# A fused gated linear attention and expert layer: the hand-laid instruction orders of its first half are laid out anew

## The chip, the core and the metric

The program runs on one core of a Trainium2 chip. The metric is the device time of one execution in microseconds (us), the median of several executions. The core has a matrix engine (TensorE, PE), a vector engine (VectorE, DVE), an activation engine (ScalarE, ACT), GpSimd (POOL) and a queue engine (SyncE, SP) that issues DMA transfers. Each takes its own instructions strictly in the order in which the program gives them, so an instruction that waits holds back all that stand behind it on its engine.

## What is computed

A gated linear attention (4 batches, 8 heads, 768 steps, head size 48) is followed by a top-1 mixture of 8 experts over the 3072 resulting tokens:

```python
mag = np.sqrt(a_re * a_re + a_im * a_im)
scale = np.minimum(mag, 0.999) / (mag + 1e-06)
a_re_n, a_im_n = (a_re * scale, a_im * scale)
for t in range(S):
    new_re = ar * S_re - ai * S_im
    new_im = ar * S_im + ai * S_re
    kv = np.einsum('bhd,bhe->bhde', k[:, :, t], v[:, :, t])
    S_re, S_im = (new_re + kv, new_im)
    y[:, :, t] = np.einsum('bhd,bhde->bhe', q[:, :, t], S_re)
...
logits = x @ w_gate
e_idx = np.argmax(logits, axis=1)
eom = 1.0 / (1.0 + np.exp(-(x @ w_output_gate)))
for e in range(E):
    mask = e_idx == e
    h = np.maximum(x[mask] @ w1[e], 0.0)
    ye = h @ w2[e]
    out[mask] = gate_w[mask, None] * eom[mask, e, None] * ye
```

## The kernel before

The kernel has two stages. **Attention and routing** work through 24 chunks of 128 tokens, six of each batch; loads and the elementwise preparation go by ten groups of 1, 1, 2, 2, 3, 3, 3, 3, 3, 3 chunks. **The experts** follow: eight of them, each with up-projections (`L1521`), a rectifier (`L1525`, `L1526`), down-projections (`L1453`, `L1479`) and the splitting of the next expert's float32 weights in a high and a low part (`L376`, `L377`).

Everything in the first stage is an operation with a name, a key (kind and chunk, `scores.21`), entered with `add_op` together with its engine and the keys that must come before it. The string `ORDER` lists all names once, and `Flow.go` emits them in that sequence; it asserts that each operation's predecessors have been emitted and that its PSUM bank is free. An engine's own order is the sequence of its names in `ORDER`. `=N` and `+N` in it put N idle multiplications on PE that compute nothing. The semaphores between the engines are derived from the data.

The names that matter, by chunk `i` or routing batch `n`:

- `scaled.i.k`, `scaled.i.q` (DVE `L783`) multiply keys and queries by the decays `ri`, `re`; `rotated.i.k`, `rotated.i.q` (DVE `L880`, tiles `kc`, `qc`) turn them by the phase. Those have two inputs in SBUF. `phase.i`, `whole.i`, `part.i`, `carry.i` sum up the phase angles from chunk to chunk (PE `L830`, `L833`; DVE `L837`, `L864`, `L823`).
- `half.i.k.0` and the like (PE `L252` on `kc`, `qc`) transpose one half of these, `copied` (ACT `L893`) empties the bank.
- `scores.i` (PE `L951`) is the product of queries and keys, `masked.i` (DVE `L957`) masks it, `values.i` (PE `L974`, `L981`) multiplies by the values and by the state of the chunk before, `xt.i` (ACT `L987`) empties that bank, `rows.i` (PE `L252` on `xt`) transposes back and `xn.i`, `stored.i` write the rows to DRAM.
- `state.i` (PE `L920`), `summed.i` (DVE `L928`), `carried.i` (POOL `L931`) carry the state on.
- `gates.m` and its steps 1 to 3 give a pair of chunks its gate logits: PE `L408`, ACT `L412`, PE `L252` on `ls`, DVE `L418`.
- The routing goes in batches of 8, 8 and 4 chunks (n = 0, 1, 2), the last four chunks apart as `place` and `place_two`. `choose.n`, `choose2.n` (DVE) find the expert of each token, `ranks.n` (PE `L455`) counts, `ranked.n` (DVE `L457`, `L459`, tile `found`) gives each token its rank, `exps.n` and `weighed.n` (ACT, then DVE `L480` to `L483`, tile `entry`) its weight. `hot.c` (`L539`) marks the ranks of chunk c, on POOL for batch 0 and on DVE afterwards. `cut.n` and `product.n` (POOL `L545` to `L552`, tiles `parts`, `rest`, `many`) split the entries, and `listed.n`, `listed.n.1` (PE `L559`) add up the two halves of a batch into one PSUM bank, which `held.n` empties.
- After batch 2, `spread` (PE `L569`), `slots` (DVE `L575`) and `first_ids` (DVE `L1360`) give the rows of the first expert, which `gather.0` to `gather.3` (POOL, DMA, `L1382`) fetch and `identity.0` to `identity.3` (PE `L1212`) transpose. `fill` and `last` (PE `L1196`) add the last four chunks; then the first up-projection starts.
- `split.0` to `split.5` (ACT and DVE) split the first weights, `raw.0` to `raw.8` load them (SP).

Of the kernel before, what the change touches and what calls it, by code (L numbers as in the profile page):

```python
# [40 lines left out]
    arctan.3 phase.2 whole.1 halves.1 v.5 wg.1 kinds part.1 k.6 magnitude.0 =3 carry.2 magnitude.1 q.6 cosine.0 sine.1
    phase.3 v.6 whole.2 cosine.1 part.2 rotated.0.q ar.6 sine.2 =3 carry.3 ai.6 magnitude.2 phase.4 whole.3 ar.7
    half.0.q.0 part.3 ai.7 half.0.q.1 copied.0.q.0 rotated.0.k ar.8 carry.4 copied.0.q.1 sine.3 ai.8 half.0.k.1
    whole.4 cosine.2 phase.5 copied.0.k.1 part.4 k.7 magnitude.3 sine.4 q.7 =1 carry.5 magnitude.4 cosine.3 ratios.0
    cosine.4 whole.5 half.0.k.0 state.0 copied.0.k.0 part.5 scores.0 sine.5 magnitude.5 scaled.1.q cosine.5
    rotated.1.k rc.0 load.1 carried.0 state.1 masked.0 half.1.k.0 ln2.2 ratios.1 summed.1 values.0 copied.1.k.0 sum.2
    half.1.k.1 rotated.1.q scale.2 k.8 copied.1.k.1 bound.2 +2 half.1.q.1 xt.0 half.1.q.0 q.8 count.2 ln2.3 decay.2
    v.7 copied.1.q.1 sum.3 ar.9 ri.2 rows.0 rc.1 ai.9 copied.1.q.0 scaled.2.k xn.0 ar.10 count.3 scores.1 ln.4 ai.10
    rotated.2.k ar.11 re.2 ai.11 inverse.4 masked.1 carried.1 +1 half.2.k.1 stored.0 decay.3 copied.2.k.1 ratio.4
    scale.3 values.1 ri.3 bound.3 square.4 scaled.2.q v.8 decay.4 xt.1 scaled.3.k ar.12 ln2.4 rotated.2.q gates.0  # L50
    ai.12 rotated.3.k row.2 k.9 gates.0.1 half.2.q.1 re.3 half.2.k.0 copied.2.q.1 sum.4 row.3 ar.13 copied.2.k.0
    half.2.q.0 ri.4 ai.13 half.3.k.0 copied.2.q.0 decay.5 ar.14 scaled.3.q scale.4 scaled.4.k ai.14 rows.1 rotated.3.q
    q.9 scores.2 ri.5 copied.3.k.0 bound.4 re.4 xn.1 row.4 half.3.k.1 re.5 half.3.q.0 scaled.4.q copied.3.k.1 decay.6
    copied.3.q.0 masked.2 halves.2 ln.5 half.3.q.1 ratios.2 q.10 rotated.4.q values.2 copied.3.q.1 row.5 stored.1
    inverse.5 count.4 ri.6 half.4.q.0 xt.2 ratio.5 state.2 copied.4.q.0 re.6 scores.3 v.9 rc.2 rotated.4.k square.5
    k.10 scaled.5.k half.4.k.1 summed.2 halves.3 ln2.5 decay.7 scaled.5.q k.11 half.4.q.1 scaled.6.q row.6 ri.7
    decay.8 scaled.6.k q.11 copied.4.q.1 sum.5 re.7 ri.8 row.7 ratios.3 copied.4.k.1 masked.3 carried.2 re.8 state.3
    scale.5 row.8 half.4.k.0 rotated.5.q gates.0.2 values.3 copied.4.k.0 load.1.5 summed.3 rotated.5.k rc.3 count.5
    half.5.q.0 arctan.4 v.10 rows.2 copied.5.q.0 bound.5 phase.6 xn.2 xt.3 state.4 arctan.5 whole.6 carried.3 scores.4
    gates.0.3 part.6 carry.7 gates.1 summed.4 masked.4 phase.7 gates.1.1 carried.4 sine.6 half.5.k.0 magnitude.6  # L60
    half.5.k.1 whole.7 halves.4 cosine.6 values.4 part.7 copied.5.k.1 sine.7 carry.8 copied.5.k.0 scaled.7.k
    magnitude.7 rotated.6.k phase.8 xt.4 rows.3 cosine.7 whole.8 half.5.q.1 xn.3 ratios.4 part.8 copied.5.q.1 q.12
    rows.4 scaled.8.k rc.4 magnitude.8 v.11 half.6.k.0 carry.9 sine.8 scores.5 k.12 rotated.6.q copied.6.k.0 stored.2
    cosine.8 rotated.7.k xn.4 stored.3 phase.9 load.2 masked.5 half.6.q.0 half.6.k.1 copied.6.q.0 decay.9 whole.9 ln.6
    half.6.q.1 scaled.7.q values.5 part.9 q.13 copied.6.k.1 rotated.7.q k.13 copied.6.q.1 inverse.6 stored.4 carry.10
# [66 lines left out]
    identity.0 identity.1 identity.2 identity.3 fill.20 place_two high.23 place_two.0 low.22 place_two.1 fill.21  # L132
    place_two.2 low.23 piece.3 place_two.3 place_two.4 hot.20 hot.21 hot.22 hot.23 tail_exps last.0 last.1 xn.22 xn.23
    first_high.0 first_low.0 last.2 first_high.1 first_low.1 first_up.0 first_high.2 first_up.1 first_low.2 stored.22
    tail_gates cut.3 product.3 first_up.2 stored.23
"""


# [1644 lines left out]
```

## Time and profile before

| what | value |
|---|---|
| median of 3 runs | 476.84 us (475.33 to 477.55) |
| profiled execution, its own time | 477.41 us |
| its span, first to last instruction | 475.2 us |
| mean granted clock of TensorE | 0.988 |
| busy: PE, DVE, ACT, POOL | 452.8, 373.5, 301.0, 131.7 us |

2.2 us lie outside the span. Times in the rows are counted from the span's start. A row of the timeline has the start, the length, engine, line, operation, tiles and, in brackets, how long the engine stood idle ahead of it and whom it waited for. A row of the windows has the length of a stretch, then each engine's busy time in it with its instructions, the granted clock (1.00 is the level of 2.4 GHz, 0.50 that of 1.2 GHz) and the load of the DMA engines.

### The profile page before, as it was taken

Reading aid. Unit: us, or ns where it says so; the run is one execution under the profiler, and the core shown is the slowest. Engines: PE = TensorE matmul, PEld = TensorE weight load, DVE = VectorE, ACT = ScalarE, POOL = GpSimd, SP = SyncE. Lnnn points to the kernel's source line nnn. Section 1 sums busy time; section 2 is a strip of 40 time slices with the busy share of each in tenths; the row PEclk is TensorE's granted clock in tenths of the full one; section 3 lists DMA queues with packets and bytes.
Section 4 is the critical chain, followed back from the end, with each engine's and each line's share of the span. In section 5 each row is a group of like instructions: output and inputs, shape, how many; then the busy total and the mean of one; then the engine's idle time right before and its main releaser. Section 6 shows DMA issues by size and latency. Waiting matters only on the chain.

```text
span 475.2 us, 13763 instructions
## 1 busy us (share of the span) xinstructions
PE 452.8 (95%) x5634; PEld 391.8 (82%) x5634; DVE 373.5 (79%) x716; ACT 301.0 (63%) x580; POOL 131.7 (28%) x169
## 2 busy tenths in 40 slices
PE   8998989999999999989899999999999999999992
PEld 7765767777776777768778899999999999999992
DVE  4799999999997999973867587595886859597540
ACT  6879989999997997644444553553626445463231
POOL 5300410023932231124014051704226060410232
PEclk9999999999999999988999999999999999999998
DMA  8946516454442220025834846373552837310111
GB/s 277 292 132 205 183 52 183 138 171 134 135 149 87 72 86 20 32 89 129 272 107 114 280 120 198 86 238 104 182 158 57 279 95 229 108 38 0 51 40 57
DMA packets 45436, 63.91 MB, mean 134 GB/s; under 512 B 10365, under 2 KB 37200, under 8 KB 45364
## 3 DMA queue, kind: packets, MB, share of 16 engines
q1 hardware_dynamic: 38132, 53.55, 35.9%
q0 software_dynamic: 7232, 9.39, 7.4%
q8 instruction: 46, 0.75, 0.7%
q14 instruction: 26, 0.21, 0.2%
HBM read 53.83 MB, written 9.77 MB: 134 GB/s over the span
## 4 chain that ended last, share of the span: by engine, by line
PE 68%; DVE 19%; ACT 5%; issue 3%; POOL 2%; DMA 2%; SPq 0%; POOLq 0%; DVEq 0%; ACTq 0%
PE up L1521 23%; PE acc L1453 20%; PE tr L252 4%; PE sx L974 3%; DVE scores L957 3%; PE sx L951 3%; PE cs L830 2%; PE sx L981 2%; DVE kc L880 2%; PE xt L252 2%; DVE qc L880 1%; PE acc L1479 1%; DMA ar<-in_a_re_blocks_dram 1%; PE tr L920 1%; DVE l L743 1%
## 5 line engine op out<-in xcount | busy, mean ns | idle before, releaser
L1525 ACT ACTIVATE hh<-up 128x384 fp32r<-128x384 f32 (+6 forms) x64 | 32.9, 513 | 91.5 <-PE up L1521 89.8
L1526 DVE SCALAR_TENSOR_TENSOR hl<-up,hh 128x384 fp32r<-128x384 f32 (+6 forms) x64 | 37.3, 583 | 46.9 <-ACT hh L1525 46.5
L1521 PE MATMUL up<-xh,w1h 128*128 128x384 f32 (+6 forms) x192 | 68.5, 357 | 0.0
L1521 PE MATMUL up<-xl,w1h 128*128 128x384 f32 (+6 forms) x192 | 67.2, 350 | 0.0
L1521 PE MATMUL up<-xh,w1l 128*128 128x384 f32 (+6 forms) x192 | 67.1, 350 | 0.0
L1382 POOL DMA_INDIRECT rows<-xd,sid x28 | 35.4, 1264 | 96.3 <-PE xt L252 78.1
L1453 PE MATMUL acc<-hh,w2h 128*128 128x464 f32 (+6 forms) x168 | 59.0, 351 | 0.0
L1453 PE MATMUL acc<-hl,w2h 128*128 128x464 f32 (+6 forms) x168 | 58.9, 351 | 0.0
L1453 PE MATMUL acc<-hh,w2l 128*128 128x464 f32 (+6 forms) x168 | 58.9, 351 | 0.0
L1466 POOL DMA_INDIRECT out_dram<-y,sid x28 | 31.5, 1125 | 48.2 <-ACT y L1491 43.3
L1487 DVE COPY y<-yt 32x384 f32<-32x384 f32 x112 | 39.8, 355 | 1.9
L951 PE MATMUL sx<-qt,kt 32*128 32x128 f32 x1152 | 39.0, 279 | 0.3 <-ACT xt L987 0.2
L951 PEld LDWEIGHTS sx<-qt,kt 32*128 32x128 f32 x1152 | 34.4, 187 | 3.3 <-issue 1.4
L1521 PEld LDWEIGHTS up<-xh,w1h 128*128 128x128 f32 x192 | 36.1, 188 | 1.1 <-issue 0.4
L1521 PEld LDWEIGHTS up<-xh,w1l 128*128 128x128 f32 x192 | 36.2, 188 | 0.8
L1521 PEld LDWEIGHTS up<-xl,w1h 128*128 128x128 f32 x192 | 36.1, 188 | 0.8
L931 POOL TENSOR_TENSOR state<-summed,rc 128x288 f32<-128x288 f32 x16 | 16.1, 1006 | 72.9 <-DVE summed L928 31.9
L377 DVE TENSOR_TENSOR w1l<-raw,w1h 128x512 fp32r<-128x512 f32 x48 | 30.4, 683 | 6.7 <-ACT w1h L376 6.5
L1453 PEld LDWEIGHTS acc<-hl,w2h 128*128 128x128 f32 x168 | 31.6, 188 | 0.9
L1453 PEld LDWEIGHTS acc<-hh,w2l 128*128 128x128 f32 x168 | 31.6, 188 | 0.8
L1453 PEld LDWEIGHTS acc<-hh,w2h 128*128 128x128 f32 x168 | 31.6, 188 | 0.8
L377 DVE TENSOR_TENSOR w2l<-raw,w2h 128x512 fp32r<-128x512 f32 x48 | 30.2, 683 | 0.2
(230 smaller groups left out, 1036.1 us busy)
## 6 DMA issues: line engine op xcount, KB each, us to landing
raw<-in_moe_w_dram SPq DMA_DIRECT2D x29, 768.0 KB, 5.4
ar<-in_a_re_blocks_dram SPq DMA_DIRECT2D x24, 192.0 KB, 4.2
ai<-in_a_im_blocks_dram SPq DMA_DIRECT2D x24, 192.0 KB, 3.4
k<-in_k_blocks_dram SPq DMA_DIRECT2D x24, 192.0 KB, 2.6
q<-in_q_blocks_dram SPq DMA_DIRECT2D x24, 192.0 KB, 4.1
v<-in_v_dram SPq DMA_DIRECT2D x24, 192.0 KB, 2.4
xd<-xn SPq DMA_DIRECT2D x24, 192.0 KB, 2.9
raw<-in_moe_w_dram SPq DMA_DIRECT2D x6, 256.0 KB
```

The costliest lines, as they stand in the source:

```text
L252: return nc.tensor.transpose(out=out, in_=in_, identity=ident[p0:p0 + n, p0:p0 + n])
L377: ins = nc.vector.tensor_tensor(out=lo[:, s], in0=raw[:, s], in1=hi[:, s].bitcast(F32), op=ALU.subtract)
L880: nc.vector.tensor_tensor(out=dst, in0=n3(at(i, n)).unsqueeze(2).broadcast_to([P, NB, 2, DB]), in1=at(i, "trig"), op=ALU.mult)
L931: return lambda: engine.tensor_tensor(out=states[cc % 2], in0=of(), in1=rc[:, i, :].unsqueeze(2).broadcast_to([P, GB, D]), op=ALU.mult)
L951: r["end", "scores"] = nc.tensor.matmul(r["sx"][:, b, u * P:(u + 1) * P], kt, qt, start=(j == 0), stop=(j == JB - 1), skip_group_check=True)
L1382: nc.gpsimd.indirect_dma_start(out=rows[0][:n, i, :], out_offset=None, in_=xd[:known], in_offset=bass.IndirectOffsetOnAxis(ap=ids[:n, i:i ...
L1453: nc.tensor.matmul(accs[kt][:, :cap], w[:, cs], a, start=(ft == 0 and s == 0), stop=(ft == FT - 1 and s == 2))
L1466: ins = nc.gpsimd.indirect_dma_start(out=out, out_offset=bass.IndirectOffsetOnAxis(ap=ids(e)[:n, i:i + 1], axis=0), in_=y[:n, :], in_offse ...
L1487: nc.vector.tensor_copy(out=y[SQ * g:SQ * g + SQ, :, QD * a:QD * a + QD], in_=yt[SQ * a:SQ * a + SQ, :, g, :])
L1521: nc.tensor.matmul(up[:, :cap], w[:, kt, :], x[kt], start=(m == 0), stop=(m == 3 * KT - 1))
L1525: nc.scalar.activation(out=hh, in_=up[:, :cap], func=AF.Relu)
L1526: nc.vector.scalar_tensor_tensor(out=hl, in0=up[:, :cap], scalar=0.0, in1=hh.bitcast(F32), op0=ALU.max, op1=ALU.subtract)
```

## The change

`ORDER` is replaced by another sequence of the same names: no operation is added, removed or given to another engine, apart from the idle multiplications (16 in all become 22). SP's own order stays the same, name by name. DVE, ACT, PE and POOL get new ones. One predecessor is added, which only fixes the order of `identity.0` to `identity.3` among themselves.

```diff
 ORDER = """
-    warm.0 load.0 ar.0 ai.0 ar.1 ln.0 ai.1 inverse.0 ratio.0 ar.2 square.0 ai.2 ln.1 ar.3 ln2.0 ai.3 inverse.1 sum.0
...
+    warm.0 load.0 ar.0 ai.0 ar.1 ln.0 ai.1 inverse.0 ratio.0 ar.2 square.0 ai.2 ln.1 ar.3 inverse.1 ai.3 ln2.0
...
                 for i in range(len(tiles)):
                     add_op(("identity", i), "PE", 0.08 * KT, due, lambda i=i: gathered(i), [
-                        ("gathered", i), ("xt", NT - 1)])
+                        ("gathered", i), ("xt", NT - 1), *([("identity", i - 1)] if i else [])])
```

Lines of the changed kernel are two higher: `L559` becomes `L561`. Three places stand here engine by engine. The first is PE at `listed.2`, the sums of the last routing batch (`many`, `hot`), before:

```order
L252 MATMUL tr<-ident,xt 128x128 x4
L920 MATMUL tr<-v,kc_174 32x48 x24
L951 MATMUL sx<-qt_180,kt_181 128x128 x24
L559 LDWEIGHTS many
L559 MATMUL cs<-hot,many 40x464
```

In the kernel before, `listed.2` stands right behind `scores.21`. On PE at the same place now:

```order
L953 MATMUL sx<-qt_180,kt_181 128x128 x24
L254 MATMUL tr<-ident,qc_171 128x128 x3
L254 MATMUL tr<-ident,xt 128x128 x4
L254 MATMUL tr<-ident,kc_172 128x128 x3
L976 MATMUL sx<-scores,v 48x128 x8
L983 MATMUL sx<-qt_180,state_175 48x128 x24
L254 MATMUL tr<-ident,kc_172 128x128 x3
L254 MATMUL tr<-ident,qc_171 128x128 x3
L561 LDWEIGHTS many
L561 MATMUL cs<-hot,many 40x464
```

Between them now stand the four halves of chunk 22, `rows.19` and `values.21`. The second place is DVE at the same batch, from `ranked.2` (`of`, `found`) on, before:

```order
L459 TENSOR_REDUCE found<-of 128x8
L539 TENSOR_SCALAR hot<-iota,found 128x464 x4
L480 TENSOR_REDUCE sm<-ex 128x4
L481 TENSOR_SCALAR en<-en 128x4
L482 SCALAR_TENSOR_TENSOR en<-sm,en 128x4
L483 RECIPROCAL entry<-en 128x4
L928 TENSOR_TENSOR summed<-tr,state_175 128x288
L880 TENSOR_TENSOR kc_172<-k,trig 128x768
L957 TENSOR_TENSOR scores<-sx,mask_91 128x1024
```

And DVE there now:

```order
L461 TENSOR_REDUCE found<-of 128x8
L541 TENSOR_SCALAR hot<-iota,found 128x464 x2
L930 TENSOR_TENSOR summed<-tr,state_175 128x288
L959 TENSOR_TENSOR scores<-sx,mask_91 128x1024
L541 TENSOR_SCALAR hot<-iota,found 128x464
L482 TENSOR_REDUCE sm<-ex 128x4
L483 TENSOR_SCALAR en<-en 128x4
L484 SCALAR_TENSOR_TENSOR en<-sm,en 128x4
L485 RECIPROCAL entry<-en 128x4
L541 TENSOR_SCALAR hot<-iota,found 128x464
L882 TENSOR_TENSOR qc_173<-q,trig 128x768
L882 TENSOR_TENSOR kc_174<-k,trig 128x768
```

`weighed.2`, which gives POOL the entries for `cut.2`, now stands behind `summed.21` and `masked.21`, and both rotations of chunk 23 follow it. The third place is PE at the two halves of the first batch's sum, `listed.0` and `listed.0.1`, before (the transposition of `ls` is `gates.5.2`):

```order
L559 MATMUL cs<-hot,many 40x464
L830 MATMUL cs<-ai,tri_t_85 128x384
L252 MATMUL tr<-ident,qc_171 128x128 x3
L252 MATMUL tr<-ident,xt 128x128 x4
L559 LDWEIGHTS many
L559 MATMUL cs<-hot,many 40x464
...
L252 MATMUL cs<-ident,ls 128x128
L974 MATMUL sx<-scores,v 48x128 x8
```

The same two halves on PE now:

```order
L561 MATMUL cs<-hot,many 40x464
L410 MATMUL tr<-xt,wg 32x128 x8
L922 MATMUL tr<-v,kc_174 32x48 x24
L976 MATMUL sx<-scores,v 48x128 x8
L254 MATMUL tr<-ident,qc_173 128x128 x3
L254 MATMUL tr<-ident,kc_172 128x128 x3
L832 MATMUL cs<-ai,tri_t_85 128x384
L922 MATMUL tr<-v,kc_172 32x48 x24
L953 MATMUL sx<-qt_180,kt_181 128x128 x24
L254 MATMUL tr<-ident,kc_172 128x128 x3
L561 LDWEIGHTS many
L561 MATMUL cs<-hot,many 40x464
```

`listed.0` has moved ahead of `gates.5`, `values.12` and `scores.13`, which now lie between the halves, and `gates.5.2` has moved far behind them, to just ahead of `values.14`. On POOL, `hot.5` now stands behind `product.0`, and `carried.13` between `hot.6` and `hot.7`.

## Rows read from the trace of the kernel before

**Rows 1.** Windows of three stretches: length, busy time of each engine, clock, DMA.

```profile
30.00:201.20 171.20, 163.81 (x3528) 123.56 (x3520) 165.98 (x272) 155.29 (x294) 43.37 (x41) 1.00 0.38 115
140.00:150.00 10.00, 9.23 (x185) 6.21 (x181) 7.28 (x12) 7.69 (x14) 3.68 (x4) 1.00 0.14 43
240.60:475.00 234.40, 225.52 (x1253) 217.89 (x1251) 162.30 (x333) 105.03 (x206) 68.51 (x63) 0.99 0.42 126
```

**Rows 2.** Timeline around the last routing batch, up to the first up-projection.

```profile
201.21 1.21 DVE L957 TENSOR_TENSOR scores<-sx,mask 128x1024 f32<-128x1024 f32 x1
...
205.33 0.22 DVE L459 TENSOR_REDUCE found<-of 128x8 f32<-128x64 f32 x1
...
207.18 0.44 DVE L928 TENSOR_TENSOR summed<-tr,state 128x288 f32<-128x288 f32 x1
207.32 0.20 POOL L545 CAST parts<-entry 128x4 bf16<-128x4 f32 x1 [7.89 <-DVE entry L483]
207.53 0.95 DVE L880 TENSOR_TENSOR kc<-k,trig 128x768 f32<-128x768 f32 x1
207.60 0.94 POOL L546 TENSOR_TENSOR rest<-entry,parts 128x4 f32<-128x4 f32 x1
...
209.68 0.96 PE L559 MATMUL cs<-hot,many 128*40 128x464 bf16 x4 [1.92 <-POOL many L552]
...
218.94 1.62 PE L951 MATMUL sx<-qt,kt 32*128 32x128 f32 x48
...
225.72 1.62 PE L951 MATMUL sx<-qt,kt 32*128 32x128 f32 x48
...
227.75 1.21 DVE L957 TENSOR_TENSOR scores<-sx,mask 128x1024 f32<-128x1024 f32 x1
...
240.46 0.38 PE L1521 MATMUL up<-xh,w1h 128*128 128x464 f32 x1
```

**Rows 3.** Windows at that wait, behind it and at a later one.

```profile
208.00:210.00 2.00, 0.32 (x2) 0.22 (x3) 1.62 (x2) 0.00 (x0) 1.78 (x5) 1.00 0.82 256
211.00:218.00 7.00, 6.93 (x83) 5.60 (x80) 2.43 (x5) 1.82 (x4) 2.03 (x2) 0.51 0.00 0
228.00:230.00 2.00, 0.98 (x16) 0.83 (x16) 2.00 (x3) 2.00 (x4) 0.00 (x0) 1.00 0.45 160
```

**Rows 4.** Timeline of DVE near 145 us: its two longest waits there.

```profile
145.10 0.29 DVE L418 TENSOR_REDUCE logits<-cs 128x32 f32<-128x128 f32 x1 [1.33 <-PE cs L252]
...
148.13 0.56 DVE L837 TENSOR_SCALAR rnd<-cs 128x384 f32<-128x384 f32 x1 [1.00 <-PE cs L830]
```

**Rows 5.** Timeline of PE and DVE ahead of the sum of the first routing batch.

```profile
136.08 0.65 PE L408 MATMUL tr<-xt,wg 128*32 128x128 f32 x16
...
138.79 1.62 PE L951 MATMUL sx<-qt,kt 32*128 32x128 f32 x48
...
140.69 1.22 DVE L957 TENSOR_TENSOR scores<-sx,mask 128x1024 f32<-128x1024 f32 x1
```

**Rows 6.** Timeline of POOL in the first routing batch: its first and last operation.

```profile
115.64 4.35 POOL L539 TENSOR_SCALAR hot<-iota,found 128x464 bf16<-128x464 f16 x2 [8.23 <-DVE found L459]
...
131.48 1.70 POOL L552 TENSOR_TENSOR many<-oh,parts 128x320 bf16<-128x320 bf16 x1
```

**Rows 7.** Timeline: the same steps of POOL and PE at other places.

```profile
171.80 0.42 POOL L545 CAST parts<-entry 128x8 bf16<-128x8 f32 x1 [2.28 <-DVE entry L483]
...
174.71 0.72 POOL L552 TENSOR_TENSOR many<-oh,parts 128x320 bf16<-128x320 bf16 x1
...
242.80 0.20 POOL L546 TENSOR_TENSOR rest<-entry,parts 128x4 f32<-128x4 f32 x1
...
248.19 0.98 PE L569 MATMUL yp<-perm,sums 40*116 40x16 f32 x8
```

**Rows 8.** Timeline row of the last gather, and the tile view's landing times of all four.

```profile
221.13 1.32 POOL L1382 DMA_INDIRECT rows<-xd,sid  x1 [0.30 <-issue]
...
DMA to landing us min/median/max: 6.3/6.9/8.0
```

More of the change, by code (lines that the diff above doesn't have):

```diff
@@ L41 @@
[L41 to L65, printed above, removed]
@@ L81 @@
-    scaled.12.q ranks.0 copied.11.k.0 rotated.11.q ri.14 state.10 xt.9 ranked.0 hot.0 hot.1 rows.8 re.14 summed.10
-    exps.0 bound.7 half.11.k.1 xn.8 scores.10 load.3.5 k.18 count.7 row.13 v.16 copied.11.k.1 q.17 gates.4 sine.12
-    row.14 stored.8 masked.10 carried.10 phase.14 gates.4.1 cosine.12 half.11.q.0 arctan.7 half.11.q.1 whole.14
-    values.10 scaled.13.k copied.11.q.0 part.14 halves.6 hot.2 hot.3 hot.4 hot.5 copied.11.q.1 sine.13 carry.15
-    magnitude.14 rotated.12.k rows.9 xt.10 phase.15 xn.9 rotated.12.q sine.14 half.12.k.1 stored.9 half.12.k.0
@@ L116 @@
-    half.20.q.0 magnitude.22 scaled.22.q rows.17 ri.23 count.9 copied.20.q.0 scores.19 re.23 xn.17 load.6.5 carried.19
-    stored.17 half.20.k.1 masked.19 hot.14 hot.15 row.23 state.20 listed.1.1 copied.20.k.1 phase.23 sine.21 summed.20
-    held.1 ranking.2 half.20.q.1 cosine.21 half.20.k.0 copied.20.q.1 values.19 whole.23 sine.22 rotated.21.q
-    copied.20.k.0 order scaled.23.q gates.8.2 xt.19 half.21.q.0 part.23 rows.18 copied.21.q.0 gates.8.3 scores.20
-    magnitude.23 rotated.21.k xn.18 sine.23 scaled.23.k stored.18 halves.9 half.21.q.1 masked.20 carried.20 gates.9
@@ L131 @@
-    place.2 +3 gates.11 place.3 rows.22 gates.11.1 place.4 gates.11.2 rows.23 high.22 gates.11.3 fourth gathered.3
[L132 to L135, printed above, removed]
+    warm.0 load.0 ar.0 ai.0 ar.1 ln.0 ai.1 inverse.0 ratio.0 ar.2 square.0 ai.2 ln.1 ar.3 inverse.1 ai.3 ln2.0
@@ new lines @@
+    summed.10 ranks.0 rotated.11.q xt.9 half.11.k.1 re.14 half.11.k.0 ranked.0 k.18 copied.11.k.1 scores.10 carry.14
+    exps.0 hot.0 row.13 v.16 copied.11.k.0 bound.7 load.3.5 q.17 half.11.q.0 row.14 hot.1 rows.8 masked.10
+    copied.11.q.0 phase.14 arctan.7 half.11.q.1 whole.14 values.10 halves.6 weighed.0 sine.12 carried.10 xn.8
+    part.14 cosine.12 hot.2 scaled.13.k stored.8 copied.11.q.1 carry.15 ratios.6 sine.13 gates.4 rotated.12.k rc.6
+    phase.15 cosine.13 hot.3 gates.4.1 rows.9 rotated.12.q xt.10 gates.4.2 half.12.k.0 xn.9 whole.15 hot.4 scores.11
@@ new lines @@
+    half.13.k.0 decay.17 copied.13.k.0 part.16 square.8 half.13.q.0 scaled.15.k listed.0 masked.12 copied.13.q.0
+    gates.5 ri.17 hot.6 scaled.15.q state.13 ln2.8 carry.17 values.12 summed.13 gates.5.1 re.17 sum.8 half.13.q.1
+    xt.12 half.14.k.0 carried.13 copied.13.q.1 phase.17 magnitude.15 count.8 hot.7 state.14 scale.8 scores.13
+    summed.14 copied.14.k.0 rotated.14.q load.4.5 half.14.k.1 masked.13 listed.0.1 k.21 copied.14.k.1 sine.15 v.19
+    half.14.q.0 whole.17 held.0 values.13 row.16 row.17 bound.8 q.20 copied.14.q.0 cosine.15 stored.11 arctan.8
@@ L136 @@
+    first_low.2 hot.20 first_up.2 tail_gates hot.21 cut.3 hot.22 hot.23 product.3
 """
```

149 lines of the change are left out of this document (90 added, 59 removed).

## The prediction

> **What bounds the kernel now.** I read the windows first. From 240.6 us to 475.0, the experts, PE is busy for 225.5 of 234.4 us at full clock [rows 1]. Nothing in that stage is reordered, so what the change does to the time is what it does to the moment at which the first up-projection starts, 240.46 us [rows 2]. Ahead of that, the windows tell two regimes. From 30 to 201.2 us DVE works for 165.98 of 171.20 us, PE for 163.81, ACT for 155.29 [rows 1]: three engines nearly full, DVE the fullest, with 5.2 us of idle time. 2.7 of these lie in one stretch, 140 to 150 us, where DVE works for 7.28 us. Behind 201.2 us DVE is no longer the bound. The timeline there shows one large disturbance: PE stands 1.92 us at `listed.2`, waiting for POOL's `many` [rows 2]. In the window of that wait PE is busy for 0.32 of 2.00 us, and in the 7 us from 211 to 218 its clock is 0.51, the level of 1.2 GHz [rows 3]. A pause of about 1 us at 228 us had no such consequence: the clock stayed 1.00 [rows 3].
>
> **The change part by part.** No operation is added, apart from six idle multiplications, and none changes its engine or its form. SP's order is the same name by name, so no transfer is issued past another one on that queue. The sum is therefore one of waits that go, move or appear.
>
> *Start-up.* The same DVE operations stand ahead of the third group's bound, in another sequence, and a chain through PE and DVE sets the pace there. I take 0, with half a microsecond to either side.
>
> *The middle, up to `masked.20` at 201.21 us.* I compared the DVE operations that stand ahead of it: they are the same set before and after. The work is the same, so only idle time can differ: at most 5.2 us can be gained [rows 1]. I look for what happens to the two largest waits. DVE waits 1.33 us for the transposition of the gate logits `ls`, and 1.00 us for `phase.18` [rows 4]. Both came from the first batch's sum: `gates.5.2` needs a PSUM bank that `listed.0` holds until POOL has made `hot.6` and `hot.7`, and PE stands in order. Now `gates.5.2` follows far behind, and over 6 us of other PE work lies between the two halves of that sum, against two `hot` of at most 2.2 us each [rows 6] and one `carried`. Both waits should go: -2.3 us.
>
> What comes late next is `scores.13`. It started at 138.79 us and its mask at 140.69 [rows 5]. `listed.0` now stands just ahead of `gates.5`, which started at 136.08; with slightly less ahead of it I put it at 135.7. Up to `scores.13` PE then has 0.9 (`listed.0`), 0.6, 0.7, 1.0, two halves of 0.4, 0.8 (`phase.17`) and 0.7 (`state.14`), together 5.3 us: start 141.0, end 142.6. DVE, with 0.7 us more in front, comes to `masked.13` at 141.4 and would wait 1.2 us. So the middle brings -2.3 + 1.2 = -1.1 us. The ends: -5.2, if no idle time were left, and +2, if `scores.13` is late by the whole 3 us of work moved ahead of it and nothing absorbs that.
>
> *The end, from 201.21 us.* DVE first. Between `masked.20` and the end of `ranked.2`, at 205.55 [rows 2], one rotation of 0.87 us is now added, and a wait of 0.16 us goes: 206.25. Two `hot` (0.5), `summed.21` (0.4) and `masked.21` (1.15) bring it to 208.3, a third `hot` and `weighed.2` (0.9) to 209.2; before, POOL could start at 207.32 [rows 2]. The five POOL operations of `cut.2` and `product.2` took 2.3 us, from 207.32 to 209.62. The same kind took 3.63 us for batch 1, from 171.80 to 175.43 [rows 7]. They now run beside two rotations with two SBUF inputs, as `rest` did when it took 0.94 us beside `kc` [rows 2] and not the 0.20 of a quiet moment [rows 7]. I take the middle, 3.0 us: `many` is there at 212.2, between 211.5 and 212.9.
>
> PE does not stand still all that time. `values.21` now precedes `listed.2`: it can start when `masked.21` ends, at 208.3, and takes 1.9 us; with the two halves behind it PE reaches `listed.2` at 211.1. The wait is 0.4 to 1.8 us, 1.1 as I take it. By the pause at 228 us that is short enough for the clock to stay [rows 3].
>
> Then PE has 0.9 us of `listed.2`. The stretch from `scores.22` at 218.94 to `scores.23` at 225.72, 6.78 us without a wait [rows 2], holds the work that now lies between `listed.2` and `scores.23`, but for `spread`, 0.98 us at full clock [rows 7], and two more halves, 0.9. That makes 0.9 + 6.78 + 0.98 + 0.9 = 9.55, and `scores.23` starts at 212.2 + 9.45 = 221.65 against 225.72: 4.1 us earlier. Its mask started 2.03 us later, at 227.75 [rows 2], because DVE stood behind the choice of the tail; now it can start 1.6 us later: 4.5 us earlier. From there to the first up-projection PE is full in both orders, with the same work. Only `gather.3` may come late: it followed `slots` by some 6 us and landed 6.3 to 8.0 us behind its issue [rows 8], so it is there at about 230.5 and `identity.3` is reached at 230.3. I charge 0.3 us and keep 1.4. The end brings -4.2 us; its ends are -5.2 (short POOL chain) and -2.5 (long chain, late gather).
>
> Two moves cost nothing, and this is what hides them. `kinds` on POOL now stands ahead of `hot.0`; POOL waited 8.23 us there [rows 6]. The gate exponentials and the marks of the last four chunks now stand behind the first up-projection's inputs; POOL's `rest` at 242.80 shifts by some 0.4 us, and PE needs the result only near 246 us. If that cover were gone, it would cost the same 0.4 us.
>
> *The sum.* 0 - 1.1 - 4.2 = -5.3 us. Against the profiled execution's own 477.41 us that is 472.1. The median of the runs, 476.84, lies 0.57 us lower, so by it 471.5. I put down 471.8.
>
> **The rivals.** *The stop at `listed.2` stays.* If both rotations block POOL, each by the 0.74 us between 0.94 and 0.20, the chain takes 2.3 + 1.5 = 3.8 us and PE waits 1.9 us: the wait after which the clock fell. The low clock cost half of 7 us, 3.5, and the wait another 0.8, so that the end gains nothing: about 476. For it speaks that `weighed.2` is now later and the rotations follow it at once; against it, that batch 1, in the full middle, took 3.63. The Trainium skill says in "SBUF — State Buffer", section "Who interferes with whom", that a VectorE instruction with two SBUF inputs and a GpSimd instruction that reads SBUF exclude each other for the whole instruction. By that rule this rival would be the rule here; the trace agrees in `rest`, 0.94 beside `kc` and 0.20 alone, and no row shows the two rotations together.
>
> *The middle gives back what the end gains.* PE has only 7.4 us of idle time from 30 to 201.2 us [rows 1], and the new order asks for much of its work earlier. Two more waits like the one at `masked.13`, at 1.2 to 2 us each, leave -5.3 + 3 = -2.3: about 475. Against it: the waits shown are few, and DVE's sequence is close to the old one.
>
> *Slower: the stop moves to `listed.0`.* It now stands ahead of `gates.5`, `values.12` and `scores.13`. POOL needs its ten operations before it, 115.64 to 133.2, 17.5 us [rows 6]; PE comes at 135.7. From 20 us of POOL on, PE stands with all of that behind it. A stop of 4 us, a fall of the clock as at `listed.2`, 3.5 us, and the end's gain of 4.2 make 480.7. Against it: POOL's operations are the same, with 2.5 us in hand.
>
> *It does more.* If DVE's idle time in the middle nearly vanishes, -5.2 and -4.2 give 467.7.
>
> **How the numbers follow.** Forecast 0.55, stop stays 0.17, middle gives back 0.13, slower 0.08, more 0.07. Half a per cent, 2.4 us, is about what a measurement of this kernel can tell from no change. Faster by more than that: 0.55 + 0.07 + half of the middle's, 0.06, is 0.68. Within it: 0.17 + 0.07 = 0.24. Slower: 0.08. The range leaves out the slower case and half of the best one: 467.5 to 477.0.
>
> **What would show it.** The step at `listed.2` is right if PE's wait for `many` is under 1.5 us and no window from 200 to 240 us shows a clock under 0.95; `scores.23` then starts 4 us earlier and the first up-projection near 235. The step in the middle is right if the waits at `gates.5.3` and `whole.18` are gone, `masked.13` waits for PE about 1 us, and `masked.20` starts near 200. The experts must take 234.7 us again. It is wrong if `masked.20` starts later than 202, if POOL's chain takes over 3.7 us, or if PE waits at `identity.3` or at `listed.0`.

## The result, and the profile after

The changed kernel takes 470.5 us (median of 4 runs, 470.06 to 470.96) against 476.97 of the kernel before in the same comparison: a ratio of 0.987, 95% interval 0.9843 to 0.9897, or 6.5 us less. In a second comparison (below, `after_again`) the ratio is 0.986, interval 0.982 to 0.989. The forecast was 471.8, with 467.5 to 477.0 around it.

The profiled execution took 470.96 us, its span 468.7 us, at a mean granted clock of 0.992; up to the last matmul the clock is 1.00, and the mean is lower only for the 9.65 us behind it. Its timeline at the places of [rows 2] (columns as there; lines are two higher):

```profile
199.42 1.21 DVE L959 TENSOR_TENSOR scores<-sx,mask 128x1024 f32<-128x1024 f32 x1
...
207.29 0.22 POOL L547 CAST parts<-entry 128x4 bf16<-128x4 f32 x1 [6.27 <-DVE entry L485]
207.37 0.95 DVE L882 TENSOR_TENSOR qc<-q,trig 128x768 f32<-128x768 f32 x1
207.59 0.79 POOL L548 TENSOR_TENSOR rest<-entry,parts 128x4 f32<-128x4 f32 x1
208.24 0.95 DVE L882 TENSOR_TENSOR kc<-k,trig 128x768 f32<-128x768 f32 x1
208.44 0.80 POOL L549 CAST parts<-rest 128x4 bf16<-128x4 f32 x1
...
209.61 0.45 POOL L554 TENSOR_TENSOR many<-oh,parts 128x160 bf16<-128x160 bf16 x1
210.12 0.96 PE L561 MATMUL cs<-hot,many 128*40 128x464 bf16 x4 [0.71 <-POOL many L554]
211.49 1.62 PE L953 MATMUL sx<-qt,kt 32*128 32x128 f32 x48
...
219.50 1.62 PE L953 MATMUL sx<-qt,kt 32*128 32x128 f32 x48
221.19 1.23 DVE L959 TENSOR_TENSOR scores<-sx,mask 128x1024 f32<-128x1024 f32 x1 [0.17 <-PE sx L953]
222.47 1.08 PE L976 MATMUL sx<-scores,v 128*48 128x128 f32 x16 [1.13 <-DVE scores L959]
...
227.84 0.52 PE L1214 MATMUL acc<-ident,rows 116*128 116x116 f32 x3
...
233.48 0.37 PE L1523 MATMUL up<-xh,w1h 128*128 128x464 f32 x1
```

`masked.20` starts at 199.42 us instead of 201.21, the first up-projection at 233.48 instead of 240.46. The stop at `listed.2` is 0.71 us instead of 1.92. Nothing waits at `identity.3` (227.84).

The windows after, in the columns of [rows 1]: the whole middle, the stretch of the old hole, and the stretch behind `listed.2`, where [rows 3] had 0.51.

```profile
30.00:199.42 169.42, 162.89 (x3583) 124.48 (x3578) 166.62 (x271) 155.81 (x297) 45.49 (x50) 1.00 0.39 121
140.00:150.00 10.00, 10.00 (x234) 7.93 (x223) 9.93 (x15) 9.42 (x17) 4.43 (x3) 1.00 0.31 101
210.00:220.00 10.00, 9.80 (x225) 7.91 (x229) 4.92 (x13) 4.29 (x11) 4.62 (x6) 1.00 0.45 126
```

DVE's idle time from 30 us to `masked.20` has gone from 5.2 to 2.8 us, the 2.7 us between 140 and 150 us to 0.07, and the clock stays at 1.00.

What the sum didn't have: the same DVE operations take longer. The windows from the start of the span to `masked.20`, first of the kernel before, then of the changed one:

```profile
0.00:201.21 201.21, 191.74 (x3729) 145.25 (x3729) 184.83 (x311) 177.37 (x332) 54.04 (x95) 1.00 0.45 138
```

```profile
0.00:199.42 199.42, 190.96 (x3743) 146.35 (x3744) 186.02 (x311) 177.93 (x335) 53.94 (x94) 1.00 0.45 141
```

311 DVE operations, 184.83 us before and 186.02 now. It is no chance of one execution: the seven profiles with the new order up to `masked.20` (`after`, `middle_new` and the five taken from the changed kernel) have 185.8 to 186.0 us there, five with the old order 184.6 to 184.8. Of the DVE operations that stand by themselves in the timeline up to there, 11 before and 12 now take over 0.15 us longer than their form usually does, 4.1 and 5.2 us in all, and every one of them overlaps an operation of POOL. The longest now is a `scaled` (0.54 us elsewhere), beside a `carried` of POOL; beside another `carried` it is a rotation (0.95 elsewhere):

```profile
119.74 1.24 DVE L785 TENSOR_TENSOR k<-k,ri 128x384 f32<-128x384 f32 x1
119.89 0.66 POOL L933 TENSOR_TENSOR state<-summed,rc 128x288 f32<-128x288 f32 x1
...
145.85 1.21 POOL L933 TENSOR_TENSOR state<-summed,rc 128x288 f32<-128x288 f32 x1 [3.53 <-PE sx L983]
146.46 1.42 DVE L882 TENSOR_TENSOR qc<-q,trig 128x768 f32<-128x768 f32 x1
```

So it fits that the new order brings DVE and POOL together at other places; no run tried it by itself. Up to `masked.20` the account is: 0.56 us less idle time up to 30 us (DVE busy 19.40 there, 18.84 before), 2.42 us less behind it, 1.19 us more work, together -1.79.

From `masked.20` to the first up-projection it is 34.06 us against 39.25, -5.19. From there to the end of the last matmul both need the same, 225.57 against 225.66 us (it starts at 458.72 and 465.79 and takes 0.33). Behind the last matmul the last output write takes 9.65 us against 9.08. -1.79 - 5.19 - 0.09 + 0.57 = -6.5.

### The profile page after: what moved, and what is told of

The parts are those of the page before. It is cut to its first block, busy times and chain, and to the rows that moved or that the text cites. A ratio compares the mean times of both kernels' runs of the same rounds, so it can differ in the third digit from the quotient of the medians.

```text
span 468.7 us, 13791 instructions
## 1 busy us (share of the span) xinstructions
PE 448.4 (96%) x5646; PEld 390.5 (83%) x5646; DVE 374.4 (80%) x716; ACT 300.5 (64%) x580; POOL 133.6 (29%) x169
## 4 chain that ended last, share of the span: by engine, by line
PE 68%; DVE 21%; ACT 4%; issue 2%; POOL 1%; DMA 1%; SPq 0%; POOLq 0%; DVEq 0%; ACTq 0%
PE up L1523 23%; PE acc L1455 20%; PE tr L254 4%; DVE scores L959 3%; PE sx L953 3%; PE cs L832 2%; PE sx L976 2%; DVE kc L882 2%; DVE qc L882 2%; DVE k L785 2%; PE xt L254 2%; PE sx L983 2%; PE acc L1481 1%; DMA ar<-in_a_re_blocks_dram 1%; PE tr L1116 1%
## 5 line engine op out<-in xcount | busy, mean ns | idle before, releaser
L933 POOL TENSOR_TENSOR state<-summed,rc 128x288 f32<-128x288 f32 x16 | 15.0, 935 | 103.2 <-DVE summed L930 35.0
```

The costliest lines, as they stand in the source:

```text
L933: return lambda: engine.tensor_tensor(out=states[cc % 2], in0=of(), in1=rc[:, i, :].unsqueeze(2).broadcast_to([P, GB, D]), op=ALU.mult)
```

## The experiments

Two theories stood against each other: that the gain is the sum of two independent parts, a hole in the middle that is filled and a stop at the end, with the fall of the clock behind it, that goes; or that the parts need each other, because a wait that is taken away in one place comes back in another. The kernels differ from the two only in the sequence of names, two of them by idle multiplications; none leaves work out. They were measured in three series, each on another chip with the kernel before beside it (medians 477.63, 478.81 and 477.12 us), so a time is set against the kernel before of its own series.

**The new end alone.**

```diff
     part.23 rows.18 copied.21.q.0 gates.8.3
-    scores.20 magnitude.23 rotated.21.k xn.18 sine.23 scaled.23.k stored.18 halves.9 half.21.q.1 masked.20
...
+    xn.18 magnitude.23 halves.9 stored.18 sine.23 rotated.21.k ratios.9 cosine.22 gates.9 rc.9 cosine.23 scores.20
...
```

> The order of the kernel before up to scores.20, and from there on the names that are left, in the sequence of the changed kernel. Theory (the parts add up, and the end's part is the stop at listed.2 with the fall of the clock behind it): masked.20 starts at 201.2 us as before, PE waits less than 1.2 us for many, no window from 200 to 240 us shows a clock under 0.95, the first up-projection starts 5.2 us earlier, near 235.3, and the time is 477.0 - 5.2 = 471.8 us. Rival (the new end only works on what the new middle has left ready): PE waits 1.5 us or more somewhere between listed.2 and identity.3, the clock falls again, and at most 2 us are gained: 475 us or more.

Measured: 475.55 us against 477.63, ratio 0.9953 (0.993 to 0.9975). The clock is 1.00 up to the last matmul and the wait at `listed.2` 0.72 us, as the theory said, but only 2.1 us are gained. `masked.20` starts at 202.16, 0.95 us late, since the seam put more ahead of `scores.20`. And the gather is late. DVE at `masked.20`, and PE at the last `identity`:

```profile
202.16 1.23 DVE L957 TENSOR_TENSOR scores<-sx,mask 128x1024 f32<-128x1024 f32 x1 [0.97 <-PE sx L951]
...
232.14 0.52 PE L1212 MATMUL acc<-ident,rows 116*128 116x116 f32 x3 [1.30 <-DMA rows<-xd,sid]
```

**A cleaner seam.**

```diff
     pools clear raw.0 load.7
-    choose2.2 rotated.22.q half.21.k.1 ranks.2 copied.21.k.1 rows.19 xt.20 ranked.2 hot.16 hot.17 hot.18 hot.19
...
+    half.21.k.1 copied.21.k.1 rotated.22.k choose2.2 state.21 xt.20 rotated.22.q ranks.2 scores.21 ranked.2 exps.2 hot.16
...
```

> As end_new, but with the seam at choose2.2, where only the halves half.21.k.1 and the rotation rotated.22.k stand on the other side in the two sequences: the order of the kernel before up to choose2.2, then the names that are left in the sequence of the changed kernel. Theory (the parts add up; end_new lost 0.95 us at its seam and 1.3 us to the late gather): masked.20 starts at 201.2 us, the first up-projection 34.1 to 35.4 us later, and the time is 477.0 - 5.2 + (0 to 1.3) = 471.8 to 473.1 us. Rival (the new end needs what the new middle has got ready): 475 us or more, as in end_new.

Measured: ratio 0.9958 (0.9939 to 0.9977), again 2.0 us. `masked.20` is on time (201.38), the wait at `listed.2` 0.71 us, the gather in time. From `masked.20` to the first up-projection (239.25) it is 37.87 us against 34.06 in the changed kernel, 3.8 more: 0.7 of them up to `listed.2`, where the seam lies (`scores.21` already starts 0.7 us later behind `masked.20`); 0.9 from there to `scores.23`, where PE waits for a copy of ACT; and 2.2 from `scores.23` on, at `values.23`. The two waits in the timeline of PE, and the window behind the second:

```profile
222.48 0.66 PE L252 MATMUL tr<-ident,xt 128*128 128x128 f32 x4 [0.75 <-ACT kt L893]
...
226.85 1.08 PE L974 MATMUL sx<-scores,v 128*48 128x128 f32 x16 [1.95 <-DVE scores L957]
```

```profile
228.00:232.00 4.00, 4.00 (x74) 3.00 (x71) 1.66 (x4) 1.47 (x5) 0.00 (x0) 0.57 0.23 82
```

PE stops for 1.95 us instead of 1.13, and the clock falls there. `masked.23` itself started 0.9 us behind the end of its `scores.23`, and the last that the profile names for it (PE's `L455`) had ended 0.7 us before. Both runs went the way of the second theory: another stop can take the place of the one at `listed.2`. But 0.95 and 0.7 us were lost at the seams, which only the experiments have, so they don't show that the end needs the new middle.

**The new middle alone.**

```diff
     gates.9 order rc.9 cosine.23
-    scores.20 scaled.23.k gates.9.1 summed.20 pools held.1 carried.20 half.21.k.1 masked.20
...
+    summed.20 held.1 scores.20 scaled.23.k half.21.q.1 masked.20 carried.20 copied.21.q.1 gates.9.1
...
```

(Against the changed kernel, whose sequence runs up to there.)

> The order of the changed kernel up to scores.20, and from there on the names that are left, in the sequence of the kernel before. Theory (the parts add up): masked.20 starts at 199.4 us, the wait of some 1.9 us at listed.2 and the clock of 0.51 behind it are there as before, and the time is 477.0 - 1.8 = 475.2 us. Rival (the middle's gain is what spares the clock, since POOL gets the weights earlier): the wait at listed.2 falls under 1.2 us and the clock stays at 1.00, and the time is 472 us or less. Rival (the middle's gain is given back): 476.5 us or more.

Measured: 474.61 us against 477.63, ratio 0.9937 (0.9911 to 0.9963), 3.0 us. `masked.20` starts at 199.56. The stop of 1.92 us at `listed.2` is back, but in this execution no fall of the clock stands behind it. It comes at the next stop, where PE pauses in the middle of the 48 matmuls of `values.23` without a releaser. The windows of the stop, of the 7 us where the kernel before had 0.51, and of the fall, and the row of that pause:

```profile
206.00:208.00 2.00, 0.10 (x4) 0.00 (x0) 1.96 (x2) 0.00 (x0) 1.78 (x5) 1.00 0.82 240
211.00:218.00 7.00, 7.00 (x157) 5.87 (x159) 3.53 (x6) 3.89 (x9) 4.53 (x3) 1.00 0.46 105
227.00:230.00 3.00, 3.00 (x50) 2.42 (x49) 1.29 (x5) 0.58 (x1) 0.00 (x0) 0.50 0.91 284
```

```profile
226.93 1.53 PE L981 MATMUL sx<-qt,state 32*48 32x128 f32 x40 [0.85 <-issue]
```

So a stop of the same length has the fall behind it in one execution and not in another.

**The clock alone: fill the stop.**

```diff
-    scores.21 listed.2 listed.2.1
+    scores.21 +12 listed.2 listed.2.1
```

> The kernel before, with twelve idle multiplications on PE directly ahead of listed.2 and nothing else: PE is busy with some 1.9 us of them (0.16 us each) while it waits for many, and listed.2 itself starts at most 0.3 us later than before. Theory (the pause is what the clock falls for): no window from 200 to 240 us shows a clock under 0.95, the 7 us at 0.51 become 3.5 us, and the time is 477.0 - 3.5 + 0.3 = 473.8 us. Rival (the clock falls for another reason, or the stage behind it waits for something else anyway, so that a fast clock only makes PE wait there): within half a microsecond of 477 us.

Measured: 475.98 us against 477.63, ratio 0.9954 (0.9935 to 0.9974), about 2 us of the 3.2 expected. The timeline of PE, and the window of [rows 3]:

```profile
207.82 2.94 PE L1114 MATMUL cs<-ident 128*128 128x128 f32 x24
210.70 0.96 PE L559 MATMUL cs<-hot,many 128*40 128x464 bf16 x4
217.19 1.62 PE L951 MATMUL sx<-qt,kt 32*128 32x128 f32 x48
```

```profile
211.00:218.00 7.00, 6.76 (x122) 5.23 (x124) 2.75 (x5) 3.17 (x8) 2.36 (x2) 1.00 0.07 8
```

The clock stays. From `listed.2` to `scores.22` it is 6.49 us instead of 9.26: the fall had cost 2.8 us there, not 3.5. The twelve multiplications are 24 instructions; they took 2.9 us, not 1.9, and made `listed.2` a microsecond late. Its 12 runs lie between 475.47 and 476.41 us, the 35 of the kernel before between 475.55 and 481.31.

**Fewer of them.**

```diff
-    scores.21 listed.2 listed.2.1
+    scores.21 +8 listed.2 listed.2.1
```

> The kernel before, with eight idle multiplications instead of twelve directly ahead of listed.2. In end_fill twelve took 2.8 us (0.23 each) and made listed.2 1.0 us late, so eight take 1.9 us, about the length of the pause. Theory (the pause there is what the clock falls for, and its price is the 2.8 us by which the stretch from listed.2 to scores.22 was longer in the kernel before than in end_fill): listed.2 starts within 0.2 us of 209.7, no window from 200 to 240 us shows a clock under 0.95, and the time is 477.0 - 2.7 = 474.3 us, 0.5 to 1.5 us under end_fill, with as little spread from run to run as end_fill. Rival (a later pause of PE takes the fall over in many runs, as in the profile of middle_new): 475.5 us or more, with a spread of several us.

Measured: 477.06 us against 478.81, ratio 0.9975 (0.9949 to 1.0001), runs from 475.69 to 480.56: the rival. `listed.2` is at 210.32 with no wait, but the clock falls behind the later stop:

```profile
230.00:233.00 3.00, 3.00 (x55) 2.42 (x45) 1.71 (x6) 0.59 (x1) 0.00 (x0) 0.50 0.88 280
```

PE stops for 1.15 us at `values.23` here and pauses again for 0.26 us within it. `end_fill` has the same stop of 1.15 us without the second pause, and no fall. So filling one stop can pass the fall on to the next; it need not.

**The hole alone.**

```diff
     copied.13.q.0 decay.16 gates.4.3 copied.13.q.1
-    masked.12 ai.23 half.13.k.0 magnitude.16 decay.17 k.20 copied.13.k.0 carry.17 ln2.8 row.15 half.14.k.1
...
+    rows.11 ai.23 k.20 ri.16 row.15 re.16 xn.11 half.13.k.0 decay.17 copied.13.k.0 scaled.15.k listed.0
...
```

> The order of the kernel before, with the stretch from masked.12 to gates.6 (about 135 to 150 us) in the sequence of the changed kernel, so that gates.5.2 stands far behind the two halves of the first batch's sum. Theory (the middle's gain is this hole): the waits of DVE at gates.5.3 (1.33 us) and whole.18 (1.00 us) go, masked.13 waits for PE 0 to 1.2 us, masked.20 starts at 199 to 200 us, the end is as before, and the time is 477.0 - 1.8 = 475.2 us, between 474.7 and 475.9. Rival (DVE's idle time only moves on, because PE or ACT set the pace there): masked.20 starts at 201 us, and the time is within half a microsecond of 477 us.

Measured: 477.62 against 477.63 us, ratio 1.0 (0.997 to 1.0031). The waits at `gates.5.3` and `whole.18` are gone, and others have come. The longest waits of DVE from 30 to 203 us (total, times, longest), and the window to `masked.20`:

```profile
DVE summed L928 <- PE tr L920: 1.7, 2, 1.1
DVE ai L726 <- ACT t L724: 0.8, 1, 0.8
```

```profile
30.00:201.68 171.68, 163.98 (x3532) 123.60 (x3532) 166.54 (x273) 155.62 (x294) 45.62 (x41) 1.00 0.38 114
```

The idle time is 5.14 us, as before. It has only moved, as the rival said: PE came to `state.13` at 137.84 us, with the decays (`L767`) and `listed.0` just ahead of it, and then the engines wait in a circle, DVE 1.09 us for PE, ACT 1.92 us for DVE, PE 0.93 us for ACT.

**The whole first routing batch.**

```diff
     phase.13 copied.9.k.0 decay.13 copied.10.q.0
-    choose.0 carried.9 square.7 half.10.k.1 whole.13 half.10.q.1 scores.9 scaled.12.k copied.10.k.1 rotated.11.k
...
+    rows.7 whole.13 part.13 choose.0 xn.7 half.10.k.1 stored.7 magnitude.12 ai.20 square.7 scores.9 scaled.12.k
...
```

> As hole_new, but with a longer stretch in the sequence of the changed kernel, from choose.0 to gates.7 (about 100 to 165 us), the whole first routing batch. Theory (the hole at 140 to 150 us is filled by work that the new order has done in advance on ACT and PE in the 40 us ahead of it): DVE's idle time from 30 us to masked.20 falls from 5.2 to 2.9 us, masked.20 starts 1 to 2.3 us earlier than 201.2, and the time is 475.2 us, between 474.7 and 476.0. Rival (the idle time only moves, as in hole_new, because it is made by the whole order from the start): idle time 5 us, time within half a microsecond of 477 us.

Measured: 476.27 us against 478.81, ratio 0.9949 (0.9922 to 0.9976), 2.4 us. `masked.20` starts at 199.52, and the window to there is

```profile
30.00:199.52 169.52, 162.76 (x3528) 123.49 (x3524) 166.50 (x272) 154.91 (x294) 48.83 (x41) 1.00 0.38 116
```

3.0 us of idle time, as expected. The sequence of these 65 us brings `masked.20` as early as the whole new middle (199.56 in `middle_new`), and that of the 15 us at the hole alone doesn't. That it is the work done ahead on ACT and PE from 100 us on is likely but not shown: the stretch also reaches 15 us behind the hole, and no run took the two sides apart.

**PE's place at the end undone.** The names of PE alone; the copies of ACT move with them, DVE and POOL stay.

```diff
-    scores.21 half.22.q.1 rows.19 half.22.k.0 values.21 half.22.k.1 half.22.q.0 listed.2 listed.2.1
+    scores.21 listed.2 listed.2.1 half.22.q.1 rows.19 half.22.k.0 values.21 half.22.k.1 half.22.q.0
```

> The changed kernel with one thing undone: on PE listed.2 and listed.2.1 stand right behind scores.21 again, ahead of the four halves of chunk 22, rows.19 and values.21; DVE and POOL keep the changed order. Theory (the place on PE is what the end's gain rests on): PE is through with scores.21 at 205.1 us and POOL's many is there at 209.5 to 210.1, so PE waits 4.4 to 5 us where the changed kernel waits 0.7, the clock falls behind that, and the time is 470.5 + 4.1 + 2.8 = 477.4 us. Rival (the new DVE order brings the gain, and the work that PE would do meanwhile is only done later without loss): 473 us or less.

Measured: 481.11 us, slower than the kernel before by a ratio of 1.0043 (1.0022 to 1.0063), 8 to 9 us above the changed one by the two ratios. The timeline of PE and the window around the stop:

```profile
210.48 1.73 PE L559 MATMUL cs<-hot,many 128*40 128x464 bf16 x4 [5.01 <-POOL many L552]
```

```profile
207.00:215.00 8.00, 4.52 (x20) 2.86 (x22) 3.11 (x9) 1.33 (x3) 3.10 (x6) 0.57 0.06 22
```

PE stops for 5.01 us (expected 4.4 to 5) and the clock falls; it falls a second time behind `values.23`, where PE stops for 1.91 us, which I had not counted. With the new order of DVE, the place of `listed.2` on PE carries the end.

**The changed kernel again.** No edit.

> The changed kernel once more, as the measure for the other three of this series on the same chip. Theory: 0.987 of the kernel before, as first measured; none of its pauses in the tail is longer than 1.2 us, so the clock falls in none of its runs before the last matmul, and its runs lie within 1 to 1.5 us of each other, where those of the kernel before lie 4 to 6 us apart. Rival (the narrow spread of the first runs was chance): a spread of 3 us or more.

Measured: 470.74 us against 477.12, ratio 0.9858 (0.9823 to 0.9894). Six runs within 0.85 us, those of the kernel before beside them within 5.1 us.

**DVE's order at the end undone.**

```diff
-    hot.16 hot.17 summed.21 masked.21 hot.18 weighed.2 hot.19 rotated.23.q rotated.23.k
+    hot.16 hot.17 hot.18 hot.19 weighed.2 summed.21 masked.21 rotated.23.q rotated.23.k
```

> The changed kernel with one thing undone on DVE: hot.18, hot.19 and weighed.2 stand ahead of summed.21 and masked.21 again; PE keeps the changed order. Theory (the late weights cost nothing, since PE is busy with values.21 and the halves meanwhile; putting them first only moves the wait of PE from listed.2 to values.21): POOL starts cut.2 about 1.5 us earlier, masked.21 and values.21 start about 0.8 us later, the wait at listed.2 goes, and the time is within half a microsecond of after_again. Rival (the delay of weighed.2 was a cost): 0.7 us faster. Rival (values.21 is on the path, with a longer pause ahead of it): 0.7 us or more slower.

Measured: 470.79 us, the same as `after_again`. `values.21` is later, and the wait at `listed.2` is gone; one pays for the other. POOL's timeline is the clearest in this study:

```profile
206.62 0.20 POOL L545 CAST parts<-entry 128x4 bf16<-128x4 f32 x1 [5.00 <-DVE entry L483]
206.90 0.20 POOL L546 TENSOR_TENSOR rest<-entry,parts 128x4 f32<-128x4 f32 x1
207.16 0.20 POOL L547 CAST parts<-rest 128x4 bf16<-128x4 f32 x1
207.44 0.21 POOL L548 TENSOR_TENSOR parts<-rest,parts 128x4 bf16<-128x4 f32 x1
207.73 0.45 POOL L552 TENSOR_TENSOR many<-oh,parts 128x160 bf16<-128x160 bf16 x1
```

Beside `masked.21`, which has one input in PSUM, the five operations take 1.56 us, the small ones 0.20 each. Beside the two rotations they take 2.77 (the first fence of the result), and one operation under each rotation is stretched to 0.8. It ends as the rotation does: 208.38 and 208.32 us, 209.24 and 209.19.

**The choice of the last four chunks at its old place.**

```diff
-    split.4 last.0 stored.23 split.5 last.1
+    split.4 hot.20 hot.21 hot.22 hot.23 tail_exps last.0 stored.23 split.5 last.1
...
-    first_high.2 tail_exps first_up.1 first_low.2 hot.20 first_up.2 tail_gates hot.21 cut.3 hot.22 hot.23 product.3
+    first_high.2 first_up.1 first_low.2 tail_gates cut.3 product.3 first_up.2
```

> The changed kernel with the choice of the last four chunks at its old place: hot.20 to hot.23 and tail_exps ahead of last.0, tail_gates, cut.3 and product.3 behind first_low.2. Theory (as predicted, the move costs and brings nothing; DVE has 0.6 us of idle time there and the first up-projection is not held up by it): first up-projection within 0.3 us of after_again, time within half a microsecond. Rival (hot.20 to hot.23, 1.0 us of DVE, push first_low and with it the first up-projections): 0.7 to 1 us slower.

Measured: 471.62 us, 0.9 us above `after_again`; the runs of the two don't overlap but for 0.1 us (471.16 to 472.14 against 470.41 to 471.26). The first up-projection starts on time (233.66), but the second part of it waits, because DVE comes later to the low parts of its input:

```profile
234.53 0.48 PE L1521 MATMUL up<-xl,w1h 128*128 128x464 f32 x1 [0.29 <-DVE xl L1228]
```

From the first up-projection to the end of the last matmul it is 226.24 us instead of 225.57. So this move isn't idle: without it, the earlier end would lose 0.7 to 0.9 us again, 0.29 of them at this wait.

**The last waits filled.**

```diff
-    hot.18 values.21 weighed.2
+    values.21 weighed.2 hot.18
...
-    listed.2 copied.22.q.0 listed.2.1 half.23.q.0 held.2
+    half.23.q.0 listed.2 copied.22.q.0 listed.2.1 held.2
...
-    first_ids values.22
+    first_ids gates.10.2 gates.10.3 place values.22
...
-    rows.20 copied.23.k.0 gathered.0 gates.10.2 xt.22 gates.10.3 rows.21 place split.2 scores.23
+    rows.20 xt.22 copied.23.k.0 gathered.0 split.2 scores.23 rows.21
```

> The changed kernel with its last waits in the tail filled: half.23.q.0 ahead of listed.2 (fills 0.5 us of the 0.71 that PE waits there), hot.18 behind weighed.2 (many 0.25 us earlier), xt.22 ahead of copied.23.k.0 and rows.21 behind scores.23 (scores.23 0.6 us earlier, and 0.6 us of work into the wait of 1.13 us at values.23), and gates.10.2, gates.10.3 and place behind first_ids, so that DVE is free for masked.23 in time. Theory (PE's waits there are on the path): PE waits 0.2 us or less at listed.2 and 0.6 us or less at values.23, the first up-projection starts 1.1 us earlier, and the time is 1.1 us under after_again. Rival (the gather of the first rows is next: identity.3 was reached 6.3 us behind the last gather's issue): PE waits at identity.3 instead, and at most 0.4 us are gained.

Measured: 470.57 us, 0.2 us under `after_again` with overlapping runs: no difference. `listed.2` waits no more but starts when it did (210.53). And ACT, then PE, stop ahead of `scores.23`, in the timeline of both:

```profile
218.85 0.59 ACT L987 COPY xt<-sx 128x512 f32<-128x512 f32 x1 [1.35 <-issue]
...
219.87 1.40 PE L951 MATMUL sx<-qt,kt 32*128 32x128 f32 x40 [1.10 <-ACT kt L893]
```

ACT's pause has no releaser in the profile; `values.22`, whose bank `xt.22` empties, had ended at 217.8. Neither theory had this.

## Why the prediction came out as it did

The time lies within the range and 1.3 us under the forecast, and the waits that were to go are gone. But the reason given for the middle was too local, and several terms were mis-sized and partly offset each other: against the profiled execution 5.3 us were predicted, and it is 6.5.

| step | predicted | changed kernel |
|---|---|---|
| start-up | 0 (±0.5) | -0.56 |
| middle, idle time of DVE that goes | -2.3 | -2.4 |
| middle, new wait at `masked.13` | +1.2 | 0 |
| the same DVE work up to `masked.20` | 0 | +1.2 |
| end, to the first up-projection | -4.2 | -5.2 |
| experts, with the last write | 0 | +0.5 |

*Start-up.* -0.56 is just outside the half microsecond. The profiles with the old start-up differ by as much among themselves: DVE is busy for 18.2 to 18.8 us up to 30 us in seven of them, for 18.8 to 19.4 in the seven with the new one.

*Middle.* The two waits went, and PE does not wait at `listed.0` (135.30 us), so the slower rival had no place. `scores.13` started at 140.39, a little ahead of the 141.0 that I had worked out (the terms listed there add up to 5.5 us, not 5.3, so it should have said 141.2), but DVE came to `masked.13` only at 142.26, not at 141.4, because more of its time now goes ahead of it than the 0.7 us I had added, 0.5 of it in an operation (`L751`, at 139.19) that takes 1.83 us instead of 1.35. So there was nobody to wait. The sentence "the work is the same, so only idle time can differ" failed: the same 311 operations took 1.19 us longer. By accident this was as much as the wait that did not come. The reason for the waits was too local, too: `hole_new` shows that moving `gates.5.2` and its surroundings alone gains nothing, `batch0_new` that the order of the 65 us around them gains it.

*End, by the trace.* Each step came in the predicted order. POOL's chain took 2.77 us against 3.0, and the wait was 0.71 us against 1.1. `masked.23` stands 21.8 us behind `masked.20`, against 22.0 worked out (a sum of 9.55 us went in there as 9.45). The gather needed no charge; `end_new` shows that it could have cost 1.3. And from `masked.23` to the first up-projection it is 12.3 us now and was 12.7, where the prediction had no difference. So the end came out at the far end of its range, -5.2. The rival in which the stop stays priced a second block of POOL at 0.74 us. Two blocks are there, but the 2.3 us of the kernel before already held one.

*The clock.* The sum starts from a profiled execution with the fall behind `listed.2` and lets it go, as if every execution of the kernel before had it. The price of 3.5 us stands in two rivals alone; `end_fill` puts it at 2.8. And the fall isn't certain. The mean granted clock of each run is recorded, and of 81 runs of the kernel before in the three series 20 have 0.989 or less, as the profiled one (0.988), and 27 have 0.994 or more. The 14 profiles tell how to read that: the five at 0.990 or less have a fall ahead of the first up-projection, the four at 0.994 or more have none up to the last matmul, and in between stand both, because the clock also falls behind the last matmul, where PE does nothing (0.60 over 9.65 us in the changed kernel, 0.74 over 9.08 in the one before). In the three series the runs at 0.994 or more lie 0.6 to 0.8 us under the median. In the last one their mean, of six, is 476.5 us, the median is 477.1, and the three runs of `after_again` at 0.994 or more have 470.9. So I estimate that in the median the falls make some 0.6 to 0.8 of the 6.4 us, and that without them the new order still gains 5.6. The profile that I argued from had the long fall, and its time was near the median because something else was short in it. The last write is one such thing: 9.08 us behind the last matmul there, 9.0 to 11.0 in the 14 profiles. The pauses without a releaser are another, none of which it shows near the end. How the runs of the kernel before without a fall spend that time can't be read, since none of them was profiled: this stays open.

With the change, as far as the runs show, the clock doesn't fall any more: it is 1.00 up to the last matmul in both profiles of the changed kernel, none of its 10 runs is under 0.992, and they lie within 1.2 us. Its stops in the tail are 0.71 and 1.13 us.

*The parts don't add up.* The end alone gives 2.0 and 2.1 us, the middle alone 3.0, the whole 6.2 to 6.8. The profiles show what the end lost of its 5.2 us: one version 1.3 to the gather and 0.95 at its seam; the other 0.7 at its seam, 0.9 around a wait for ACT and 2.2 at a stop of 1.95 us with the clock behind it. The sum of the parts is 1.1 to 1.8 us short of the whole, and a seam alone costs 0.7 to 0.95. So how far the parts need each other, beyond what cutting the sequence in two costs, stays open.

*The moves that cost nothing.* The tail's choice behind the first up-projection costs nothing, as said; that it would cost 0.7 to 0.9 us to leave it where it was, I had not seen. `kinds` on POOL was not tried by itself.

*Experts.* 225.6 us of PE work from the first up-projection to the last matmul, as before; the 0.5 us lie behind it, in the last write.

## What to carry to other kernels

A wait is a symptom: rearranging the 15 us where it shows only moved it and gained nothing, and rearranging the 65 us around it gained it all. A stop that is removed can be followed by another one of the same size, so list all stops of the tail before pricing one. The same operations of an engine need not take the same time in another order: here 1.2 us of the idle time that went came back as longer operations. And a fall of the clock in one profile is one draw: look at the mean clock of all runs for how often it happens before it goes into a sum.
